# Expert matmuls as four column strips while attention runs

## The chip, the cores and the metric

The kernel runs on one core of one Trainium2 chip. The metric is the device time of one execution in microseconds (us), the median of several runs. TensorE (PE in the profile) multiplies matrices: a weight load puts a block into its 128x128 array, a matmul streams columns through it and writes to PSUM, the accumulation memory. The array can also be used as several smaller tiles side by side: in the text *full* is the whole array (128x128), *rows* are four tiles of 32x128, *columns* are four tiles of 128x32, and there are eighths of 32x64 and 64x32. VectorE (DVE) and ScalarE (ACT) do elementwise work, GpSimd (POOL) and SyncE (SP) mainly issue transfers (DMAs).

## The reference

Attention over 8 batches, 12 heads, 448 tokens and 64 dimensions of a head, followed by one expert layer over all 3584 tokens:

```python
scores = scale * np.matmul(q, k.transpose(0, 1, 3, 2))
scores = scores - np.max(scores, axis=-1, keepdims=True)
attn = np.exp(scores)
attn = attn / (np.sum(attn, axis=-1, keepdims=True) + 1e-09)
attn_out = np.matmul(attn, v)
...
x = attn_out.transpose(0, 2, 1, 3).reshape(B * S, H * D)   # 3584 x 768
h = x @ w_in                                               # 768 x 2048
g = h * (1.0 / (1.0 + np.exp(-h)))
out = g @ w_out                                            # 2048 x 768
```

## The kernel before, in words

**Units.** Attention is cut into units of one batch and four heads (three groups of heads a batch); batch 0 is cut once more, into pieces of 224 query tokens, so its first units are half as wide. For a unit, `scores` (L339, matmul at L327) makes the transposed scores of keys against queries on row tiles, the head in the row position; ACT takes the exponential (`expo`, L364); `attend` (L414) multiplies the exponentials by ones, which gives the sums, and by V, in column tiles with the head in the column position (matmuls at L390 and, for sums of a pair of units, L406). DVE inverts the sums and writes the scaled result as `xT` (L473), the expert layer's input with the model dimension on the partitions.

**Expert layer.** `ffn1` (L484, matmul at L487) makes one block of 128 hidden units for all tokens of a piece: six matmuls that accumulate over the model dimension, 224 columns wide for the two pieces of batch 0 and 448 for the later batches. ACT takes tanh, DVE forms the gate `G` (L533). `plain` (L695, matmul at L699) and `product` (L675, matmul at L685) multiply `G` by `w_out` in matmuls of 384 columns; `product` belongs to a scheme for pairs of token blocks that needs seven products in place of eight, with sums and differences made by DVE (L671, L746). The last two batches have the same scheme for `w_in`: `pair_product` (matmul at L622), which comes after attention. All these matmuls use the full array.

**Order.** The order on PE, ACT and DVE is not written out by hand. The class `Order` (L78) is a planner that runs while the kernel is built: it keeps a clock, books each operation with an assumed duration, and at each step starts what is ready by its rules. Scores go first, one burst each `PACE` (2.6), the value passes and expert operations fill the time between them; rings stand for buffers. The operations are then recorded in that order, so a change of an assumed duration can change the order. `on_pe` (L106) adds `SWITCH` (0.094) to an operation whose `mode` (the tile) differs from the one before it; `run_qk` names its mode "rows" or "rest rows", `run_av` "cols" (and leaves "rest cols" behind after a pair of units), expert operations "full". Until the first expert operation PE multiplies zeros in idle time (`run_zeros`, L1434), with `warm["on"]` set.

**Program.** Each matmul is recorded with a weight load of its own. The built program has 3,679 matmuls on PE and 7,407 instructions in all there. PE's instructions come from memory over a DMA queue of their own (queue 8 in the profile).

Of the kernel before, what the change touches and what calls it, by code (L numbers as in the profile page):

```python
# [25 lines left out]
def mm(n):  # L26
    return n / 2400.0 + 0.0026
# [6 lines left out]
class Ring:  # L34


    def __init__(self, n):
        self.free = [0.0] * n
# [26 lines left out]
class Op:  # L65


    def __init__(self, eng, busy, emit, deps=(), bias=0.0, tail=HOP, then=None):
        self.eng, self.busy, self.emit = eng, busy, emit
        self.deps, self.bias, self.tail, self.then = list(deps), bias, tail, then  # L70
        self.done = None
        self.half = False

    def ready(self):
        return when(self.deps)


class Order:  # L78


    def __init__(self, shy):
        self.now, self.shy = 0.0, shy
        self.free = {"PE": 1.0, "ACT": 2.1, "DVE": 1.2, "POOL": 1.2}
        self.wait = {"ACT": [], "DVE": []}
        self.pool = []
        self.dma_free = 0.0
        self.out = []
        self.mode = None
        self.busy = {e: 0.0 for e in self.free}

    def add(self, op):
# [4 lines left out]
        self.out.append((self.now, len(self.out), fn))  # L96

    def start(self, op):
        self.emit(op.emit)
        self.free[op.eng] = self.now + op.busy  # L100
        self.busy[op.eng] += op.busy
        op.done = self.now + op.busy + op.tail
        if op.then:
            op.then(op.done)

    def on_pe(self, op, mode):  # L106
        gap = SWITCH if mode != self.mode else 0.0
        self.mode = mode
        op.busy += gap
        self.start(op)  # L110
# [55 lines left out]
def kernel(  # L166
# [9 lines left out]
    nc = tc.nc  # L176
# [135 lines left out]
    def turn_q(n):  # L312
        t = rawq[n][:].bitcast(FP32).rearrange("p (g i) -> p g i", i=32)
        nc.vector.transpose(out=t, in_=t)  # L314
        QT[n] = rawq[n].rearrange("p (q e) -> p e q", e=2)

    def score_banks(n, w, ys):
        for y in ys:
            pS_t[(n, w, y)] = ps.tile(
                [128, 2, 512], FP32, name=f"s_{n}_{w}_{y}", tag="s", bufs=2  # L320
            )
# [139 lines left out]
    def x3(b, cc):  # L461
        if (b, cc // 3) not in xT:
            xT[(b, cc // 3)] = sb.tile(
                [128, 3, S], FP16, name=f"xT_{b}_{cc // 3}", tag="xT", bufs=NX3
            )
        return xT[(b, cc // 3)]
# [17 lines left out]
    def ffn1(b, f, t0, t1):  # L484
        h = ps.tile([128, 512], FP32, name=f"h_{b}_{f}_{t0}", tag="m", bufs=4)
        for cc in range(NDC):
            nc.tensor.matmul(  # L487
                out=h[:, 0 : t1 - t0],
                lhsT=w_in_t[:, cc, 128 * f : 128 * (f + 1)],
                rhs=x3(b, cc)[:, cc % 3, t0:t1],  # L490
                start=(cc == 0),
                stop=(cc == NDC - 1),
            )
        h_t[(b, f, t0)] = h
# [87 lines left out]
    def w_in_part(i, j, f0, f1):  # L582
        at = DFF // 2 * j
        return w_in_t[:, 3 * i : 3 * i + 3, at + 128 * f0 : at + 128 * f1]
# [18 lines left out]
    def pair_product(f, m):  # L603
        if m in (1, 5):
            pp_t[(f, PBANK[m])] = ps.tile(
                [128, 512], FP32, name=f"f_{f}_{m}", tag="m", bufs=4
            )[:, 0:S]
        elif m == 6:
            two = ps.tile([128, 2, 512], FP32, name=f"f_{f}_{m}", tag="s", bufs=2)
            pp_t[(f, "B")], pp_t[(f, "D")] = two[:, 0, 0:S], two[:, 1, 0:S]  # L610
        x = {(r, i): x3(PB + r, 3 * i) for r in range(2) for i in range(2)}
        lo, at = f // 4 * 4, slice(128 * (f % 4), 128 * (f % 4 + 1))
        a, w = {
            1: (x[0, 0], w_in_part(0, 0, f, f + 1)),
            2: (x[0, 1], w_in_part(1, 0, f, f + 1)),
            3: (sx_t.get(4), w_in_part(1, 1, f, f + 1)),
        }.get(m, (None, None))
        if a is None:
            i = {4: 4, 5: 1, 6: 2, 7: 3}[m]
            a, w = x[1, 1] if m == 4 else sx_t[i], tw_t[(i, lo)][:, :, at]  # L620
        for c in range(3):
            nc.tensor.matmul(  # L622
                out=pp_t[(f, PBANK[m])],
                lhsT=w[:, c, :],
                rhs=a[:, c, :],
                start=(c == 0 and m in (1, 6, 5)),
                stop=(c == 2),
                skip_group_check=True,
            )
# [45 lines left out]
    def product(qd, m):  # L675
        a, b = 2 * qd, 2 * qd + 1
        if m in (5, 6):
            w = S_t[(qd, m - 4)]
        else:
            t, i = {1: (a, 0), 2: (a, 1), 3: (a, 1), 7: (b, 0), 4: (b, 1)}[m]  # L680
            w = rows(t, i)
        if BANK[m] == m:
            pr_t[(qd, m)] = ps.tile([128, 512], FP32, name=f"p_{qd}_{m}", tag="m", bufs=4)
        for f in range(HF):
            nc.tensor.matmul(  # L685
                out=pr_t[(qd, BANK[m])][:, 0:OH],
                lhsT=w[:, f, :],
                rhs=W_[m][:, f, :],
                start=(f == 0 and BANK[m] == m),
                stop=(f == HF - 1),  # L690
                skip_group_check=True,
            )


    def plain(t, j, f0, f1):  # L695
        if f0 == 0:
            pr_t[("o", t, j)] = ps.tile([128, 512], FP32, name=f"o_{t}_{j}", tag="m", bufs=4)
        for f in range(f0, f1):
            nc.tensor.matmul(  # L699
                out=pr_t[("o", t, j)][:, 0:OH],  # L700
                lhsT=rows(t, f // HF)[:, f % HF, :],
                rhs=B_[f // HF, j][:, f % HF, :],
                start=(f == 0),
                stop=(f == NFF - 1),
                skip_group_check=True,
            )
# [56 lines left out]
    od = Order(SHY)  # L763
# [476 lines left out]
    qk_seq, av_seq = [], []  # L1240
# [191 lines left out]
    warm = {"on": 1, "first": 1}  # L1432
# [10 lines left out]
    while True:  # L1443
        plan_turns(qk_seq[0][0][0] + 3 if qk_seq else NU)
        plan_adds()
        plan_pair()
        plan_sums()
        soon = od.step()
        if od.free["PE"] <= od.now:
            ran = False  # L1450
            moe_i, moe_next = moe_ready()
            av_data["at"] = None
            qk, av = qk_at(), av_at()
            wait = av_data["at"]
            if wait is not None and wait <= od.now - 1000 and not (av is not None and av <= od.now):
                moe_i, moe_next = moe_ready(0)
                soon.append(min([x for x in m_ring.free if x>od.now] or [od.now+0.1]))
            near = qk_seq and units[qk_seq[0][0][0]][0] == 0 and qk is not None
            near = near and qk < od.now + NEAR
            if qk is not None and qk <= od.now and (od.now >= pace["next"] or moe_i is None):  # L1460
                u0 = units[qk_seq[0][0][0]]
                pace["next"] = min(max(pace["next"], od.now - 4), od.now) + (
                    PACE if u0[0] > EAGER else 0.0
                ) * len(qk_seq[0][2]) / 2
                run_qk()
                od.now, keep = od.free["PE"], od.now
                while u0[0] and (a := av_at()) is not None and a <= od.now:
                    run_av()
                    od.now = od.free["PE"]
                od.now = keep  # L1470
                ran = True
            elif near:
                pass
            elif moe_i is None and av is not None and av <= od.now:
                run_av()
                ran = True
            elif moe_i is not None:
                if av is not None and av <= od.now - 0:
                    run_av()
                else:  # L1480
                    moe.pop(moe_i)[2]()
                ran = True
            if not ran:
                soon += [x for x in (moe_next, qk, av, pace["next"]) if x is not None]
        soon.append(od.free["PE"])
        later = [x for x in soon if x > od.now]
        if not later:
            break
        wait = min(later) - od.now
        if warm["on"] and od.free["PE"] <= od.now and wait > 0.06 and od.now > 0.9:  # L1490
            each = mm(128) if od.now > COLD else 0.107
            n = max(1, int((wait - 0.06) / each), int(wait / each + 0.9) * (od.now < COLD))
            if warm.pop("first", None):
                n = FIRST
            od.on_pe(Op("PE", n * each, lambda n=n: run_zeros(n)), "full")
        od.now = min(later)
        assert od.now < 2000.0
# [33 lines left out]
```

## Time and profile before

| | |
|---|---|
| median of 3 runs | 396.07 us (395.69 to 396.17) |
| the profiled execution | 396.11 us |
| its span | 394.3 us |
| TensorE clock granted | 1.00 |
| PE busy | 387.6 us |
| DVE, ACT, POOL busy | 272.7, 253.6, 83.6 us |
| DMA packets | 35,579, 34.43 MB |

The span is the time from the first to the last instruction that the profiler saw. Busy time of PE is modelled: matmuls overlap, so their starts tell more than their durations; "x32" after a group counts its instructions. "PEld" are weight loads. A wait's releaser is what ended it; "issue" means that nothing in the profile did. The DMA share is the mean busy share of 16 DMA engines, and may read a little above one.

The four costliest groups of PE, by line and tile (busy us, mean ns of one, idle time before them):

```
L487 PE MATMUL h<-xT,w_in_t 128*128 128x448 f16 x480 | 98.9, 353 | 0.0
L685 PE MATMUL p<-w_out_t,G 128*128 128x384 f16 x368 | 65.3, 326 | 0.3 <-DVE xT L473 0.2
L685 PE MATMUL p<-D,S 128*128 128x384 f16 x208 | 37.4, 327 | 0.0
L327 PE MATMUL s<-rq,KT 32*128 32x448 f16 x496 | 36.0, 360 | 0.1
```

### The profile page before, as it was taken

What the parts mean: (1) busy time and instruction counts of PE and PEld (TensorE: products, weight loads), DVE (VectorE), ACT (ScalarE), POOL (GpSimd) and SP (SyncE); (2) the same over time, 40 slices, a digit from 0 to 9 for tenths busy, and PEclk for the clock granted to TensorE, in tenths of its full rate; (3) what the DMA queues carried; (4) which work ended last, traced back from release to release, by engine and by line L of the source; (5) the groups of instructions that cost most, each with busy time, mean ns of one, the idle gap of its engine ahead of it and who ended that gap; (6) DMA issues with size and microseconds to landing.
All of it is one profiled execution on the core that took longest, in us unless ns stands there. A gap on an engine that the chain in (4) does not pass through costs nothing.

```text
span 394.3 us, 9242 instructions
## 1 busy us (share of the span) xinstructions
PE 387.6 (98%) x3679; PEld 200.0 (51%) x3679; DVE 272.7 (69%) x570; ACT 253.6 (64%) x404; POOL 83.6 (21%) x153
## 2 busy tenths in 40 slices
PE   8999999999999999999999999999999999999995
PEld 7667764443444444554444444444444555555563
DVE  2466676999967588963698576896879945457332
ACT  4988885696871986753974759867685236763221
POOL 7532547215001532330006131600000000000000
PEclk9999999999999999999999999999999999999999
DMA  7999999919033946292016683711100130001343
GB/s 116 204 210 210 162 179 187 154 35 141 13 65 79 148 56 86 50 193 62 2 23 90 116 162 52 98 24 31 51 2 7 33 99 25 2 1 29 95 110 90
DMA packets 35579, 34.43 MB, mean 87 GB/s; under 512 B 11600, under 2 KB 34000, under 8 KB 35536
## 3 DMA queue, kind: packets, MB, share of 16 engines
q0 software_dynamic: 24784, 22.82, 38.7%
q1 hardware_dynamic: 9984, 10.24, 9.6%
q10 hardware_dynamic: 768, 0.79, 0.8%
q8 instruction: 29, 0.48, 0.5%
q14 instruction: 14, 0.11, 0.1%
HBM read 45.61 MB, written 11.01 MB: 144 GB/s over the span
## 4 chain that ended last, share of the span: by engine, by line
PE 91%; DVE 4%; ACT 1%; DMA 1%; issue 1%; ACTq 0%; POOL 0%; DVEq 0%; POOLq 0%
PE p L685 28%; PE h L487 28%; PE s L327 12%; PE a L390 10%; PE f L622 8%; PE o L699 3%; PE a L406 2%; DMA rq<-in_q_dram 1%; DVE tw L598 1%; ACT E L364 1%; PE z L1438 1%; DVE G L533 1%; ACTq L734 0%; DVE S L671 0%; DVE G L671 0%
## 5 line engine op out<-in xcount | busy, mean ns | idle before, releaser
L364 ACT ACTIVATE E<-s 128x896 f16<-128x896 f32 (+1 forms) x172 | 149.9, 915 | 22.6 <-PE s L327 21.2
L487 PE MATMUL h<-xT,w_in_t 128*128 128x448 f16 (+1 forms) x672 | 118.9, 327 | 0.0
L487 PEld LDWEIGHTS <-w_in_t 128*128 128x128 f16 x672 | 61.1, 98 | 54.4 <-issue 18.8
L498 ACT ACTIVATE th<-h 128x448 f16<-128x448 f32 (+1 forms) x112 | 54.3, 495 | 31.6 <-PE h L487 21.5
L533 DVE SCALAR_TENSOR_TENSOR G<-th,h 128x448 f16<-128x448 f16 (+2 forms) x112 | 55.1, 507 | 16.0 <-ACT th L498 14.0
L685 PE MATMUL p<-w_out_t,G 128*128 128x384 f16 x368 | 65.3, 326 | 0.3 <-DVE xT L473 0.2
L685 PEld LDWEIGHTS <-G 128*128 128x128 f16 x472 | 45.3, 98 | 33.4 <-issue 4.0
L269 POOL DMA_DIRECT2D V<-in_v_dram x88 | 48.6, 570 | 57.1 <-PE a L390 43.6
L327 PE MATMUL s<-rq,KT 32*128 32x448 f16 (+4 forms) x864 | 56.7, 340 | 0.6 <-ACT E L364 0.4
L742 ACT COPY ost<-p 128x384 f32<-128x384 f32 x39 | 18.7, 479 | 48.5 <-PE p L685 33.5
L390 PE MATMUL a<-E,V 128*32 128x448 f16 (+3 forms) x864 | 40.6, 335 | 0.0
L473 DVE SCALAR_TENSOR_TENSOR xT<-a,rdn 128x448 f16<-128x448 f32 (+1 forms) x54 | 28.9, 568 | 12.5 <-PE a L390 11.7
L254 POOL DMA_DIRECT2D rq<-in_q_dram x27 | 15.2, 561 | 105.2 <-PE s L327 85.8
L685 PE MATMUL p<-D,S 128*128 128x384 f16 x208 | 37.4, 327 | 0.0
L327 PEld LDWEIGHTS <-KT 32*128 32x128 f16 (+2 forms) x864 | 17.5, 98 | 28.7 <-issue 25.9
L390 PEld LDWEIGHTS <-V 128*32 128x32 f16 (+2 forms) x864 | 18.2, 95 | 22.6 <-issue 15.3
L375 DVE TENSOR_TENSOR T<-T,E 128x1792 f16<-128x1792 f16 x20 | 21.7, 1086 | 11.4 <-ACT E L364 11.4
L685 PEld LDWEIGHTS <-S 128*128 128x128 f16 x208 | 19.4, 98 | 16.2 <-issue 3.1
L375 DVE TENSOR_TENSOR T<-E,E 128x1792 f16<-128x1792 f16 x20 | 21.7, 1083 | 7.8 <-ACT E L364 7.8
L647 ACT ACTIVATE G<-f 128x448 f16<-128x448 f32 x32 | 16.2, 547 | 8.4 <-PE f L622 8.3
L304 DVE STREAM_TRANSPOSE KT<-rk 128x256 f32<-128x256 f32 (+3 forms) x48 | 16.6, 384 | 5.9 <-DMA rk<-in_k_dram 5.8
L314 DVE STREAM_TRANSPOSE rq<-rq 128x448 f32<-128x448 f32 (+1 forms) x27 | 15.3, 570 | 6.0 <-DMA rq<-in_q_dram 5.9
(124 smaller groups left out, 323.6 us busy)
## 6 DMA issues: line engine op xcount, KB each, us to landing
out_dram<-ost SPq DMA_DIRECT2D x208, 48.0 KB, 1.6
rk<-in_k_dram POOLq DMA_DIRECT2D x24, 224.0 KB, 4.9
rq<-in_q_dram POOLq DMA_DIRECT2D x21, 224.0 KB, 5.2
w_in_t<-in_moe_w_in_dram POOLq DMA_DIRECT2D x6, 512.0 KB, 11.6
w_out_t<-in_moe_w_out_dram POOLq DMA_DIRECT2D x4, 768.0 KB, 12.9
V<-in_v_dram POOLq DMA_DIRECT2D x43, 64.0 KB, 3.8
V<-in_v_dram POOLq DMA_DIRECT2D x40, 48.0 KB, 3.6
out_dram<-ost ACTq DMA_DIRECT2D x16, 48.0 KB, 1.8
```

The source lines that it names most:

```text
L269: nc.gpsimd.dma_start(out=VT[b][32 * x : 32 * (x + 1), hs, 0:count, :], in_=v[b, hs].rearrange("h (i g) d -> i h g d", g=TPP)[:, :, first ...
L327: nc.tensor.matmul(out=pS[p0 : p0 + 32 * (x1 - x0), h % 2, at : at + nq], lhsT=KT[(b, hg)][32 * h : 32 * (h + 1), c, x0:x1, :, e], rhs=QT[ ...
L364: nc.scalar.activation(out=E[(n, w)][0:kr, 2 * y : 2 * y + 2, 0:nk], in_=pS_t[(n, w, y)][0:kr, :, 0:nk], func=AF.Exp, scale=attn_scale,)
L375: nc.vector.tensor_tensor(out=T[n], in0=T[n] if step else E[(n, 0)], in1=E[(n, step + 1)], op=ALU.add,)
L390: nc.tensor.matmul(out=a[32 * h : 32 * (h + 1), 0:nq], lhsT=w, rhs=e[k0:k1, h, at : at + nq], start=start, stop=stop,)
L473: nc.vector.scalar_tensor_tensor(out=x3(b, cc)[:, cc % 3, 32 * g0 : 32 * g1], in0=acc[(n, part)][:, 0:nq], scalar=0.5, in1=rdn_t[n].rearra ...
L487: nc.tensor.matmul(out=h[:, 0 : t1 - t0], lhsT=w_in_t[:, cc, 128 * f : 128 * (f + 1)], rhs=x3(b, cc)[:, cc % 3, t0:t1], start=(cc == 0), s ...
L498: nc.scalar.activation(out=th, in_=h_t[(b, f, t0)][:, 0 : t1 - t0], func=AF.Tanh)
L533: nc.vector.scalar_tensor_tensor(out=dst[:, f, at + lo : at + hi], in0=th_t[(b, f, t0)][:, lo - t0 : hi - t0], scalar=1.0, in1=h_t[(b, f, ...
L622: nc.tensor.matmul(out=pp_t[(f, PBANK[m])], lhsT=w[:, c, :], rhs=a[:, c, :], start=(c == 0 and m in (1, 6, 5)), stop=(c == 2), skip_group_ ...
L685: nc.tensor.matmul(out=pr_t[(qd, BANK[m])][:, 0:OH], lhsT=w[:, f, :], rhs=W_[m][:, f, :], start=(f == 0 and BANK[m] == m), stop=(f == HF - 1),
L742: nc.scalar.copy(out=ost(qd, i, j), in_=bank(qd, m))
```

## The change

A helper `wide` issues a matmul either as it was or as four, each with a quarter of the stationary columns and of the output partitions, on 128x32 tiles; all four stream the same operand, and together they do the same arithmetic. It takes the place of the matmul in `ffn1`, `pair_product`, `product` and `plain`. An operation gets its `strips` mark in `on_pe`: when its mode is "full" and attention work is left (`od.attention`, set anew at each step of the planner), the mode becomes "cols", so that the planner books no change of tile between it and a value pass. When the operations are recorded, `run` sets the flag that `wide` reads. The order is drawn anew with these modes.

```diff
@@ class Op
         self.done = None
         self.half = False
+        self.strips = False
@@ class Order
         self.out = []
         self.mode = None
+        self.strips = False
+        self.attention = True
         self.busy = {e: 0.0 for e in self.free}
...
     def start(self, op):
-        self.emit(op.emit)
+        self.emit(lambda: self.run(op))
...
+    def run(self, op):
+        self.strips = op.strips
+        op.emit()
+
     def on_pe(self, op, mode):
+        if mode == "full" and self.attention:
+            mode, op.strips = "cols", True
         gap = SWITCH if mode != self.mode else 0.0
         self.mode = mode
         op.busy += gap
...
+    def wide(out, lhsT, rhs, **flags):
+        n = 4 if od.strips else 1
+        for j in range(n):
+            at = slice(128 // n * j, 128 // n * (j + 1))
+            nc.tensor.matmul(out=out[at], lhsT=lhsT[:, at], rhs=rhs, **flags)
+
@@ ffn1; the same in pair_product, product and plain
         for cc in range(NDC):
-            nc.tensor.matmul(
+            wide(
                 out=h[:, 0 : t1 - t0],
                 lhsT=w_in_t[:, cc, 128 * f : 128 * (f + 1)],
                 rhs=x3(b, cc)[:, cc % 3, t0:t1],
@@ the planner's loop
         plan_pair()
         plan_sums()
+        od.attention = bool(qk_seq or av_seq) and not warm["on"]
         soon = od.step()
```

More of the change, by code (lines that the diff above doesn't have):

```diff
@@ L621, in pair_product @@
         for c in range(3):
-            nc.tensor.matmul(
+            wide(
                 out=pp_t[(f, PBANK[m])],
@@ L684, in product @@
         for f in range(HF):
-            nc.tensor.matmul(
+            wide(
                 out=pr_t[(qd, BANK[m])][:, 0:OH],
@@ L698, in plain @@
         for f in range(f0, f1):
-            nc.tensor.matmul(
+            wide(
                 out=pr_t[("o", t, j)][:, 0:OH],
```

## The prediction

> **What bounds the kernel now.** I read the busy shares first, then the chain of waits, then TensorE's waits and timeline, and last the DMA queues and the packets of one of them.
>
> ```profile
> PE 387.6 (98%) x3679; PEld 200.0 (51%) x3679; DVE 272.7 (69%) x570; ACT 253.6 (64%) x404; POOL 83.6 (21%) x153
> ...
> PE 91%; DVE 4%; ACT 1%; DMA 1%; issue 1%; ACTq 0%; POOL 0%; DVEq 0%; POOLq 0%
> ...
> q8 instruction: 29, 0.48, 0.5%
> ```
>
> TensorE (PE) is busy 98% of the 394.3 us span and is 91% of the chain that ended last; the next engine has 31% to spare. So a microsecond taken from or put on PE is a microsecond of the time. The view of PE's waits agrees: four entries, 2.1 us together. The last line is queue 8, which brings PE's own program: 0.48 MB in 29 packets of 16,384 bytes; the built program has 7,407 PE instructions, so a packet holds 256 of 64 bytes.
>
> What the change aims at is in PE's timeline around 70 us (start, duration, what):
>
> ```profile
> 67.92 1.47 PE L699 MATMUL o<-w_out_t,G 128*128 128x384 f16 x8
> 69.32 1.63 PE L390 MATMUL a<-E,V 128*32 128x448 f16 x32
> 70.89 0.58 PE L327 MATMUL s<-rq,KT 32*128 32x448 f16 x8
> 71.39 0.82 PE L699 MATMUL o<-w_out_t,G 128*128 128x384 f16 x4
> ```
>
> Starts are to be compared with starts. Eight matmuls of 384 columns take 8 x 0.1626 = 1.30 us (0.1626 us is the start-to-start time within such a run), yet the value pass starts 1.40 us after them: 0.10 us went to the change of tile. The four-matmul run at 71.39 starts 0.50 us after the scores, whose two rounds need 0.38 and some 0.02 us of their own: 0.10 us again. I took the same difference at every change of tile in the trace. Medians in ns: full to rows (32x128, scores) 96, rows to full 107, full to columns (128x32, values) 93, columns to full 106, rows to columns 102, columns to rows 106, columns to 64x32 103, 64x32 to full 127, 64x32 to columns 124. Which two tiles meet hardly matters; how often they change does.
>
> The third thing is a place where PE waited for nothing that another engine did (timeline of PE, and the busy time of PE in three stretches with clock, DMA share and GB/s):
>
> ```profile
> 27.39 0.56 PE L390 MATMUL a<-E,ones 128*32 128x224 f16 x13
> 28.43 0.28 PE L390 MATMUL a<-E,ones 96*32 96x224 f16 x3 [0.49 <-issue]
> ```
>
> ```profile
> 16.87:22.24 5.37, 5.37 (x132) 1.00 1.13 210
> 22.24:28.43 6.19, 5.71 (x134) 1.00 1.13 211
> 28.43:34.48 6.05, 6.04 (x127) 1.00 1.13 210
> ```
>
> Sixteen matmuls belong to one pass; 13 run, and the last three come 0.65 us late in the middle of a group of four, released by "issue". The packets of queue 8 around it started at 19.85, 26.02 and 32.12 us and took 0.95, 0.95 and 0.94 us. Late in the kernel packets start when PE has run some 170 to 190 instructions past a multiple of 256; the stall sits at instruction 962, which is 194 past one. So I read it as a block boundary: PE had run out of program, and the packet that ended at 26.97 us ended the stall 1.47 us later. From the stall's end (PE enters the new block and asks for the next) to the next packet's start are 3.69 us. One round of supply is thus 3.69 + 0.94 + 1.47 = 6.1 us for 256 instructions. The three stretches are the blocks there: 5.37, 6.19 and 6.05 us. The kernel before touches this limit only here, where scores and value passes of 224 columns stand close together; later its blocks last 10 to 24 us, since a full-array matmul of 448 columns is two instructions in 0.189 us.
>
> **The change part by part.**
>
> Array time. Four strips of 128x32 in four column groups should take the time of one full matmul. The value passes show it: in the run at 69.32 the groups of four start 0.189 us apart, as full matmuls of 448 columns do. I cost 480 + 480 matmuls of 448 and 384 columns at no change. The 186 matmuls of 224 columns become groups of four that the first value passes run at 95 to 100 ns against 96: 0 to +0.7 us; I take 0, because in those stretches the supply below decides.
>
> Changes of tile. Counted in the two built orders: 259 before, 236 after. Between expert work and value passes 40 changes (14 + 12 + 14) become 4, but 64x32 to columns rises from 5 to 18, and around scores nothing is saved: full-rows pairs turn into columns-rows pairs. With the medians above (neighbours where a pair is new) the sums are 26.9 and 25.0 us: **-1.9 us**. The bounds by the cheapest and dearest row, 23 x 0.089 and 23 x 0.127, are -2.0 and -2.9; I take -1.9, pair by pair.
>
> The redrawn order. Up to about 60 us the orders agree; later the same work is shifted by a few operations, and attention runs up to 2 us earlier against the pair sums of w_out. No step is added on ACT, DVE, POOL or SP; POOL's and SP's issues have the same counts. The wait of PE that a new order can win or lose is bounded by the 3.5 us that all waits and late starts cost before: I take 0, with -1 to +2 for the range.
>
> Instructions. This is the dear part. PE's program grows from 7,407 to 14,283 instructions (3,438 matmuls more, each with its weight load), so 56 packets instead of 29. The 0.44 MB are nothing beside 34.43 MB; their rate matters. I cut the new order into blocks of 256 and gave each its array time from the rows above. Until 28.4 us the order is the old one, stall included. Then follow the first two sets of expert matmuls, 224 columns wide, where a group of eight instructions needs only 0.096 us. The nine blocks from there need 4.43, 3.50, 3.50, 4.18, 3.50, 3.50, 4.36, 4.84 and 5.15 us of array time, 37.0 together. At 6.1 us a block the supply needs 54.9: +17.9 us. Nothing covers it: PE is what sets the end, and exponentials and gates are only late with it. The page has the DMA engines at 9 tenths until 79 us, so the 6.1 us measured in that load applies at first; but the stretch now lasts from 28 to some 80 us with the same bytes to load. Behind it a block (eight instructions per 0.163 or 0.189 us, plus scores and changes of tile) needs 5.3 to 6.6 us, and the DMA share falls from 1.13 to 0.45 (80 to 280 us). The shortest round that I can read is that of the packets at 12.27 and 19.85 us: each starts 2.98 us after PE passed the boundary, 2.98 + 0.95 + 1.47 = 5.4 us. So I take 0 for the later blocks, with +2.1 if the round stayed at 6.1. For the early ones I let the last four rounds be 5.4 us: 17.9 - 4 x 0.7 = **+15.1 us**. Bounds, each block's shortfall added up: 5.0 us throughout, an estimate a little below the shortest, gives +7; 6.4 gives +20.
>
> [...]
>
> Sum: -1.9 + 15.1 = +13.2, span 394.3 to 407.5. That execution took 396.11 us, 1.8 us around its span, beside a median of 396.07. So 409.3: **409 us**.
>
> **The rivals.**
>
> An issue floor instead of late blocks: PE's sequencer cannot pass a matmul with its load faster than the densest stretch, 5.37 us / 132 = 41 ns. Groups of four then last at least 163 ns: nothing for 448 and 384 columns, 186 x 0.067 = +12.5 us for 224. With -1.9 that is 406.7. For it: no stretch of several us is denser. Against it: shorter runs are (112 instructions in 1.6 us, 29 ns a matmul), and the stall came in one piece.
>
> [...]
>
> No limit of supply: the 0.65 us was a single accident, and blocks are fetched far enough ahead. Then only the changes of tile count: 396.1 - 1.9 = **394.2 us**, faster. For it: one visible stall in 29 packets. Against it: three rounds in a row that all come out near 6 us, and a stall on a boundary. It would decide if a round were under 3.5 us.
>
> The strips don't run at once, since all four stream the same operand: each group would take four times as long, hundreds of us. Four value strips stream four different operands at full rate, so I see no reason.
>
> **How the numbers follow.** Late blocks 0.79 (own range 401 to 418), issue floor 0.07, no limit 0.11, strips in series 0.01, and 0.02 for a small loss of supply that cancels the gain. What this kernel's measurement can tell from no change is about 0.2%, 0.8 us. Faster 0.11; same 0.02; slower 0.87. The range takes the late blocks with their bounds and the issue floor: 396.1 - 1.9 + 7 = 401 to 396.1 - 1.9 + 20 + 2 + 2 = 418.
>
> **What would show it.** PE's busy count near 7,117 matmuls and queue 8 at about 56 packets. Right, if between 28 and 85 us PE has gaps of 1 to 3 us released by "issue" every 256 instructions, packets of queue 8 some 6 us apart, and expert work there takes 12 to 18 us longer, while behind it the two kernels run side by side. Evenly spread groups of 163 ns without gaps would be the issue floor. No gaps, and a value pass starting straight behind strips without its 0.1 us, would be the second rival. Wrong in size, if the rounds are 5 us or reach into the later stages.

## The result, and the profile after

The changed kernel takes 407.36 us (median of 4 runs, 405.36 to 408.87) beside 395.88 us of the kernel before in the same runs: a ratio of 1.0283, 95% interval 1.0259 to 1.0308. It is slower, as forecast, by 11.5 us where 13 were forecast. The profiled execution is the shortest of the four, 405.36 us with a span of 403.6.

The page of the changed kernel; the lines answer to those shown of before (busy time, chain by engine, PE's program queue):

```profile
PE 387.0 (96%) x7117; PEld 209.6 (52%) x7117; DVE 273.5 (68%) x570; ACT 253.1 (63%) x404; POOL 83.6 (21%) x153
...
q8 instruction: 55, 0.90, 1.0%
...
PE 89%; DVE 4%; issue 3%; ACT 1%; DMA 1%; ACTq 0%; DVEq 0%; POOLq 0%
```

PE works as long as before (387.0 against 387.6 us), with nearly twice as many matmuls; the span is 9.3 us longer, and "issue" has grown from 1% to 3% of the chain. PE's program now comes in 55 packets instead of 29. Where the time went is in the timeline of PE, changed kernel, in the stretch of the 224-column strips (start, duration, what, count, idle time before):

```profile
34.30 0.85 PE L330 MATMUL h<-xT,w_in_t 128*32 128x224 f16 x26 [1.22 <-issue]
35.09 0.57 PE L342 MATMUL s<-rq,KT 32*128 32x448 f16 x8
35.59 2.48 PE L330 MATMUL h<-xT,w_in_t 128*32 128x224 f16 x94
40.23 0.85 PE L330 MATMUL h<-xT,w_in_t 128*32 128x224 f16 x26 [2.16 <-issue]
```

At 35.59 us 94 strips run back to back, at 0.096 us for four, the spacing of one full-array matmul of 224 columns in the kernel before. Then PE stands still for 2.16 us in the middle of a group of four (94 and 26 are 120, five operations of 24), and nothing that another engine did releases it. Scores are hit in the same way:

```profile
57.72 0.57 PE L342 MATMUL s<-rq,KT 32*128 32x448 f16 x6
60.90 0.37 PE L342 MATMUL s<-rq,KT 32*128 32x448 f16 x2 [2.61 <-issue]
```

I counted PE's matmuls and weight loads up to each such place, and measured each against the undisturbed spacing of its row. There are seven between 27 and 66 us, of 0.39, 1.39, 2.33, 2.30, 0.47, 2.78 and 0.74 us, 10.4 us together. They stand behind instructions 961, 1217, 1473, 1729, 2241, 2497 and 2753 of PE, 256 or 512 apart; so in each, PE stops after instruction 193 or 194 of a block of 256, and it goes on 1.30 to 1.55 us after the end of a packet of queue 8. The kernel before has one, of 0.65 us, at the same count.

What the change was to save is saved. Timeline of PE, changed kernel:

```profile
78.51 0.83 PE L330 MATMUL o<-w_out_t,G 128*32 128x384 f16 x16
79.17 1.62 PE L405 MATMUL a<-E,V 128*32 128x448 f16 x32
```

Four groups of 384 columns need 4 x 0.1626 = 0.65 us, and the value pass starts 0.66 us after them. Before, it started 0.10 us later than its work explained. At 21 places of this trace where strips and a pass on 128x32 tiles meet, in either order, the median of the extra time is 0.00 us.

The account of the two profiled executions (405.36 - 396.11 = 9.25 us): stalls on program 10.4 - 0.65 = +9.7; changes of tile -1.9 by count and medians; a wait of the pair products of w_out for xT near 316 us 1.23 instead of 0.32, +0.9; the first scores, near 6 us, wait for the transposed queries 0.65 us instead of 0.26, but start only 0.10 us later than before, +0.1. Together +8.8; some 0.4 us are not accounted for.

### The profile page after: what moved, and what is told of

Same layout as the page of the kernel before. It is cut to its first block, busy times and chain, and to the rows that moved or that the text cites. A ratio compares the mean times of both kernels' runs of the same rounds, so it can differ in the third digit from the quotient of the medians.

```text
span 403.6 us, 16126 instructions
## 1 busy us (share of the span) xinstructions
PE 387.0 (96%) x7117; PEld 209.6 (52%) x7117; DVE 273.5 (68%) x570; ACT 253.1 (63%) x404; POOL 83.6 (21%) x153
## 4 chain that ended last, share of the span: by engine, by line
PE 89%; DVE 4%; issue 3%; ACT 1%; DMA 1%; ACTq 0%; DVEq 0%; POOLq 0%
PE p L330 27%; PE h L330 27%; PE s L342 12%; PE a L405 10%; PE f L330 8%; PE o L330 3%; PE a L421 1%; DMA rk<-in_k_dram 1%; ACT E L379 1%; DVE tw L613 1%; PE z L1453 1%; DVE G L548 1%; DVE S L686 1%; DVE G L686 0%; DVE xT L488 0%
## 5 line engine op out<-in xcount | busy, mean ns | idle before, releaser
L330 PE MATMUL h<-xT,w_in_t 128*32 128x448 f16 (+2 forms) x2670 | 120.1, 327 | 6.1 <-issue 6.1
L330 PEld LDWEIGHTS <-w_in_t 128*32 128x32 f16 (+1 forms) x2742 | 72.9, 97 | 62.4 <-issue 22.3
L330 PEld LDWEIGHTS <-G 128*32 128x32 f16 (+1 forms) x1544 | 53.8, 97 | 37.8 <-issue 7.6
L330 PE MATMUL p<-w_out_t,G 128*32 128x384 f16 (+1 forms) x1016 | 65.2, 326 | 1.2 <-DVE xT L488 1.1
L263 POOL DMA_DIRECT2D rq<-in_q_dram x27 | 15.1, 558 | 116.4 <-PE s L342 102.3
L330 PE MATMUL p<-D,S 128*32 128x384 f16 (+1 forms) x568 | 37.4, 326 | 0.0
L330 PEld LDWEIGHTS <-S 128*32 128x32 f16 (+1 forms) x568 | 20.9, 97 | 13.7 <-issue 1.6
L330 PE MATMUL p<-D,G 128*32 128x384 f16 (+1 forms) x272 | 19.1, 326 | 0.0
```

The lines of the kernel that those rows point to most:

```text
L330: nc.tensor.matmul(out=out[at], lhsT=lhsT[:, at], rhs=rhs, **flags)
```

## The experiments

Eleven kernels. Those that keep the changed kernel's order differ from it only where the diff says so.

### The order alone

Strips are booked, and every matmul is recorded on the full array:

```diff
     def run(self, op):
-        self.strips = op.strips
+        self.strips = False
         op.emit()
```

> The redrawn order of the changed kernel, but every expert matmul on the full array again: 3,679 matmuls, 258 changes of tile (before 259). Late blocks of program (my theory: PE's instructions come in blocks of 256, one about every 6 us while the DMA engines are loaded, and the strips of 224 columns use a block up in 3.5 us): no block is shorter than in the kernel before, so 395 to 397.5 us; up to 1 us more than before is the order's own, since the changed kernel has one wait of 1.1 us for xT near 316 us that before has at 0.2. Rival, the order is what costs: 404 us or more.

Measured 396.72 us, ratio 1.0020 (1.0011 to 1.0030). The redrawn order costs 0.8 us and not 11. PE's waits in this kernel (engine, line, what it waited for: us in total, times, longest) name the place:

```profile
PE p L330 <- DVE xT L488: 0.9, 1, 0.9
```

The kernel before has the same entry at 0.2: the last product before `pair_product` comes earlier than its input.

### The strips alone, in the order before

```diff
     def on_pe(self, op, mode):
         if mode == "full" and self.attention:
-            mode, op.strips = "cols", True
+            op.strips = True
```

> Strips as in the changed kernel, but the planner books them as full, so that the order is that of before; 7,093 matmuls, 236 changes of tile. Late blocks: -1.9 us of changes of tile, some 8 to 12 us of stalls at instruction 193 or 194 of a block between 28 and 70 us: 402 to 408 us. Rival, the order is what costs: 394 us.

Measured 405.90 us, 1.0258 (1.0237 to 1.0278): the loss is there without the new order. Stalls stand again at 193 or 194 of a block, 8.1 us in six of them. The built program has 236 changes of tile too, so the new order had saved no change of tile. Its profile shows a second cost, in the section on the hardware below.

### Strips only where they are wide, and only where they are narrow

The changed kernel's order. `op.narrow` is set in `queue_ffn1` for the pieces of 224 tokens; the second kernel has `and op.narrow`.

```diff
     def run(self, op):
-        self.strips = op.strips
+        self.strips = op.strips and not op.narrow
         op.emit()
```

> The changed kernel's order; strips for the matmuls of 448 and 384 columns (3,840 strips in 960 groups), full array for the 186 of 224 columns, so PE's program is 13,100 instructions long instead of 14,283 and 239 changes of tile are left. Late blocks: the blocks under 5 us are gone (shortest behind 60 us 5.2), so the 10.4 us of stalls are nearly gone: 394.5 to 397 us, below the kernel before by up to 1.6 unless the order's wait takes it back. Rival, each strip costs a little wherever it stands: 84% of the loss stays, about 405 us.

> The complement: the changed kernel's order, strips for the matmuls of 224 columns alone (744 strips), everything else on the full array: 4,237 matmuls, 257 changes of tile. Late blocks: seven blocks of 3.5 to 4.4 us from 28 us on, shortfall to a 6.1 us round 16.0 us, to the rounds that the changed kernel had about 9: 402 to 408 us, with a stall at instruction 193 or 194 of nearly every block. Rival, each strip costs a little: 16% of the loss, 398.5 us.

Wide strips alone: 395.20 us, 0.9985 (0.9977 to 0.9994), a little below the kernel before, with 3,840 of the 4,584 strips of the changed kernel. Narrow strips alone, the other 744: 408.16 us, 1.0301 (1.0287 to 1.0315), just above the expected stretch. So the whole loss belongs to a sixth of the strips, and a price on each strip is refuted. The timeline of PE in the kernel with narrow strips alone:

```profile
36.24 2.48 PE L331 MATMUL h<-xT,w_in_t 128*32 128x224 f16 x94
40.87 1.49 PE L331 MATMUL h<-xT,w_in_t 128*32 128x224 f16 x26 [2.16 <-issue]
```

The same 94 strips and the same 2.16 us as in the changed kernel: later strips have no part in it. The wide ones use up 256 instructions in 5.2 us at the least, and no stall on program stands in their stretch.

### Strips only where they meet a value pass

A pass over the finished order turns a run of strips back to the full array when neither neighbour is on 128x32 tiles; the number of changes stays 236. `od.pe` lists each operation of PE with the tile ahead of it and behind it; the lines that fill it are left out here.

```diff
...
+    i = 0
+    while i < len(od.pe):
+        j = i
+        while j < len(od.pe) and od.pe[j][0].strips:
+            j += 1
+        if j > i and od.pe[i - 1][2] != "cols" and od.pe[j][1] != "cols":
+            for x in od.pe[i:j]:
+                x[0].strips = False
+        i = j + 1
```

> The changed kernel's order; a run of expert operations is issued as strips only where it stands next to a value pass on 128x32 tiles, elsewhere on the full array: 236 changes of tile as in the changed kernel, but 4,669 matmuls instead of 7,117. Late blocks: one block of 4.4 us near 28 us costs about 1.5 us, the rest is 5.4 us or more: 394 to 396.5 us. Rival, each strip costs a little: 29% of the loss, 397.5 us. Rival, fewer changes of tile are worth nothing: 396 to 398.

Measured 396.05 us, 1.0000 (0.9991 to 1.0009). By count and medians it saves 2.2 us of changes of tile. It gives back 0.8 us for the order, and its profiled run has one stall of 1.4 us at 32.8 us, at instruction 193 of a block: narrow strips beside a value pass of batch 0 were left. (The stall at 28.4 us, 0.65 us in the kernel before, is 0.15 here.) Some 0.5 us that should be left over are not accounted for. The time lies in the stretch of the theory and in that of the second rival, so this run alone doesn't tell whether fewer changes of tile are worth anything; the next two do.

### Both lessons together

Order of before and no narrow strips; in the second kernel also only runs that meet a value pass.

> Strips for the matmuls of 448 and 384 columns alone, recorded in the order of the kernel before (the planner books them as full): 239 changes of tile, 1.6 us less than before by the medians; no block under 5.15 us. Late blocks, and the order's own loss of 0.8 us: 394.3 us (393.8 to 394.9), 0.9 below the same strips in the new order. Rival, the rest of the gain is eaten by something in the strips themselves: 395 us or more.

> Order of before; strips only in runs next to a value pass and none of 224 columns: 4,417 matmuls, 238 changes of tile, 2.0 us less than before by the medians, no block under 5.5 us but those of before. Late blocks: 393.9 us (393.4 to 394.6), as the strips that touch no value pass saved nothing. Rival, the saving of a change of tile is less than its median gap: 395 us.

Wide strips in the old order: 394.85 us, 0.9966 (0.9954 to 0.9978), at the upper end of what was expected. Only those that touch: **394.26 us, 0.9951 (0.9938 to 0.9964)**, below both kernels. Of 2.0 us expected by the medians 1.9 came. With 3,808 strips instead of 984 the gain is 0.6 us smaller. Of this 0.4 us were expected by the medians (1.6 against 2.0): going from columns to the rows of the scores takes 106 ns in the trace of before where going from the full array takes 96, and many of the added strips meet scores. The other 0.2 us is within the intervals. The profiled execution of the faster kernel is not one of its typical ones: it took 398.09 us, and the last section shows at what clock. The saving at one place, timeline of PE with wide strips in the old order:

```profile
67.69 1.48 PE L331 MATMUL o<-w_out_t,G 128*32 128x384 f16 x32
69.00 1.62 PE L406 MATMUL a<-E,V 128*32 128x448 f16 x32
```

The value pass starts 1.31 us after the eight products; in the kernel before it was 1.40.

### Is it the DMA traffic?

Dense strips deep in the kernel, where little is transferred: the kernel before with `ffn1` of batch 3 alone in strips of 224 columns, eight in place of one matmul, so that six blocks last 3.3 to 5.1 us.

```diff
         for cc in range(NDC):
+            for x0 in (t0, t0 + S // 2) if b == DENSE else (t0,):
+                x1 = x0 + S // 2 if b == DENSE else t1
+                for j in range(4 if b == DENSE else 1):
+                    p0, p1 = (32 * j, 32 * (j + 1)) if b == DENSE else (0, 128)
                     nc.tensor.matmul(
-                out=h[:, 0 : t1 - t0],
+                        out=h[p0:p1, x0 - t0 : x1 - t0],
...
-                start=(cc == 0),
+                        start=(cc == 0 and x0 == t0),
```

> The kernel before, with the expert matmuls of batch 3 alone (near 180 to 205 us, where the DMA share is about 0.45) issued as strips of 224 columns, eight in place of one: 4,351 matmuls, 261 changes of tile. Six blocks of 3.3 to 5.1 us in a stretch with light DMA traffic. If a round takes 6.1 us whatever the traffic: 36.6 - 23.2 us and less what the queue holds ahead, +11 to +13: 407 to 409 us. If the round is set by the DMA traffic (my theory): rounds of 3.5 to 5 us, 0.5 to 1.5 us a block, 398 to 402 us, with stalls again at instruction 193 or 194 of a block.

> The kernel before with the expert matmuls of batch 3 as strips of 224 columns, without added traffic (dense_light once more, with the accumulation of both halves begun once; dense_light lost the first of six terms in half of its columns). Control for the next two: 396.6 us, no stall inside a group between 175 and 210 us, packets of queue 8 some 3.6 us apart there.

The first has `start=(cc == 0)` for both halves and so leaves out the first of six terms in half of its columns; it issues the same matmuls. Measured 396.64 us, 1.0009 (0.9999 to 1.0019), and 396.49 us, 1.0011 (1.0001 to 1.0021). I had expected 398 to 402 of the first, so it is a miss: there are no stalls at all. Packets of queue 8 come every 3.5 to 4.2 us there and PE never waits. A round of 6 us is thus no constant.

Then the missing ingredient was added, 32 copies on SP's queue to output rows that are overwritten later, to the kernel before and to the dense one:

```diff
         h_t[(b, f, t0)] = h
+        if b == 3:
+            r0 = 6 * S + 128 * (f % 7)
+            for c0 in (0, OH):
+                nc.sync.dma_start(
+                    out=out[r0 : r0 + 128, c0 : c0 + OH],
+                    in_=moe_w_out[128 * f : 128 * (f + 1), c0 : c0 + OH],
+                )
```

> The kernel before, with 32 copies of 196 KB from w_out to rows of the output that are overwritten later, issued on SP's queue about where batch 3's expert matmuls stand. Control for what the traffic alone does: blocks last over 10 us there, so no late block; 396 to 399 us, the stores behind the copies being late.

> Both: batch 3's expert matmuls as strips of 224 columns, and the copies. If traffic on the DMA engines is what makes a round of supply long: stalls of 1 to 3 us at instruction 193 or 194 of a block while the copies run (DMA share near 1), packets of queue 8 5 to 7 us apart, 3 to 10 us above the larger of the two controls. If the early stretch is special for another reason: no stalls, and no more than the sum of both controls.

Measured 398.24 us, 1.0052 (1.0035 to 1.0070), and 401.35 us, 1.0121 (1.0102 to 1.0140): 3.1 us above the larger control and 2.6 above the sum of both extra times. PE at the same place, first dense strips alone, then with the copies:

```profile
196.25 0.60 PE L328 MATMUL s<-rq,KT 32*64 32x448 f16 x16
196.78 2.48 PE L492 MATMUL h<-xT,w_in_t 128*32 128x224 f16 x96
199.20 0.57 PE L328 MATMUL s<-rq,KT 32*128 32x448 f16 x8
```

```profile
196.15 0.60 PE L328 MATMUL s<-rq,KT 32*64 32x448 f16 x16
196.69 0.95 PE L492 MATMUL h<-xT,w_in_t 128*32 128x224 f16 x32
198.92 1.33 PE L492 MATMUL h<-xT,w_in_t 128*32 128x224 f16 x48 [1.28 <-issue]
```

And PE in ten-microsecond stretches (length, busy time and instructions, clock, DMA share, GB/s), again first without and then with the copies:

```profile
185.00:195.00 10.00, 10.00 (x366) 1.00 0.07 19
195.00:205.00 10.00, 10.00 (x344) 1.00 0.17 27
```

```profile
185.00:195.00 10.00, 10.00 (x370) 1.00 0.57 157
195.00:205.00 10.00, 8.40 (x288) 1.00 0.54 135
```

Same instructions, same place; with the DMA engines at 0.54 to 0.57 instead of 0.07 to 0.17 PE stops twice, for 1.45 and 0.49 us, both times at instruction 194 of a block and 1.43 and 1.33 us after the end of a packet. From PE's entry into a block to the start of the next packet passed 0.2 to 0.7 us in the six dense blocks from 186 us on without the copies; with them it was up to 2.4 us. The copies on the full-array kernel give no such stall. That traffic makes the round long is shown; the packets before these two stalls came 4.5 to 4.9 us after the ones ahead of them, not 5 to 7. The two stalls are 1.9 of the 2.6 us. Beside them value passes wait for ACT's output buffers in both kernels (1.0 us in the control, 1.4 with the strips), and scores wait 1.2 us more for exponentials; together that is more than 2.6, so how much each adds stays open.

## Why the prediction was right, and where it was off

**Direction and mechanism** held. The time of 407.36 us lies 1.6 us below the forecast, inside its own range. PE sets the end; the stalls stand on block boundaries, "released by issue", in the stretch that was named, and behind it the kernels run side by side but for the wait for xT. The signs held in part: the gaps end at 66 us and not 85, one boundary among them has none, the packets there came 3.4 to 6.7 us apart, and the stalls behind 28.4 us add up to 10 us where 12 to 18 were named. That the number came so close is partly luck. The largest term was 5.4 us too large, and 3.0 us that were not in the sum (1.0 us of waits, and 2.0 us between the profiled run and the median) made up for more than half of it.

**Array time.** Right: four strips last as long as one full matmul, at 224 columns too (0.096 us in the runs of 94).

**Changes of tile.** Right: -1.9 us by count, and the two kernels with the old order and no more late blocks than before gained 1.3 and 1.9 us. The saving needed no new order. The bounds beside it were misread: the cheapest change in the prediction's list is 93 ns, not 89, which gives -2.1 and not -2.0.

**The redrawn order.** Taken as 0 with -1 to +2; it costs 0.8 us (`order_only`).

**Instructions.** The mechanism was right and the size off. The step was 6.1 us for five rounds and 5.4 for four, +15.1 us; the profiled run had +9.7. The nine blocks from 28.4 us lasted 5.95, 5.92, 5.92, 4.13, 4.15, 6.47, 5.30, 4.80 and 5.20 us. So 6.1 was well measured for the first three, and wrong as a constant afterwards. (Its lower bound was added up wrongly too: the shortfalls to 5.0 us a block make 8.2 us, not 7.) PE in stretches of the changed kernel (length, busy, instructions, clock, DMA share, GB/s):

```profile
28.36:46.15 17.79, 12.28 (x384) 1.00 1.17 205
46.15:54.33 8.18, 7.97 (x256) 1.00 0.91 120
54.33:66.20 11.87, 8.59 (x255) 1.00 1.20 199
66.20:75.00 8.80, 8.80 (x227) 1.00 0.23 35
```

The last two columns go with the rounds: 5.9 us at a share of 1.17, short enough for blocks of 4.1 us at 0.91 and 120 GB/s, 5.3 to 6.5 at 1.20, and no stall at 0.23. The share alone tells little: with the copies, packets came 4.5 to 4.9 us apart at only 0.54 to 0.57, but at 135 to 157 GB/s. I had taken the DMA load from the page as 9 tenths up to 79 us. The tenths hide a lull that the kernel before has in the same place:

```profile
46.15:54.33 8.18, 8.11 (x103) 1.00 0.95 127
```

So two of the blocks that were given 6.1 us could have been seen to stand in lighter traffic. Only from 66 us on do the two kernels differ in load (before: 1.02, 188 GB/s).

**What was not in the sum.** The profiled run has 2.0 us less than the median, and it is the only one of the four at a granted clock of 1.00; the others show 0.99. The last section shows what such a clock can come from; for these three runs it isn't shown.

**The rivals.** The issue floor is refuted: groups of 224 columns run at 0.096 us, which is 24 ns a matmul, and the loss is in gaps. The same row refutes strips that run one after the other. "No limit of supply" is refuted for the change as it stands, and is what the kernels without narrow strips look like, 394.26 us at best against the 394.2 of that rival. That blocks are fetched far enough ahead holds for the wide strips, at 395.2 us with blocks of 5.2 us and more and no stall among them; it fails for the narrow ones, with stalls of up to 2.8 us for blocks of 3.5.

## What to carry to other kernels

Here instructions had to be fetched: the narrow strips alone, 744 at equal array time, made the 396.72 us of `order_only` into 408.16. Where a rewrite multiplies instructions at equal array time, divide the new order into blocks (256 instructions here, one packet of 16,384 bytes) and compare each block's time with the spacing of the program queue's packets under that stretch's DMA load. Read that load in GB/s over windows as short as a few blocks; here the tenths of the page hid a lull to 127 GB/s. The stalls counted here, with "issue" as releaser and in the middle of a group or pass, all at instruction 193 or 194 of a block, were late program and no dependency: in the changed kernel each ended 1.30 to 1.55 us after the end of a packet. And a saving that is made at a boundary should be paid for at that boundary only: strips next to value passes brought the gain (394.26 us with 984 strips), the others brought instructions and no gain that these runs can tell (394.85 with 3,808).

## What the runs showed of the hardware that was not expected

Behind some waits of PE the granted clock halved. PE in four stretches of 3.4 us, kernel with the strips in the old order (clock is the third figure behind the stretch):

```profile
34.40:37.80 3.40, 3.40 (x128) 1.00 1.16 210
37.80:41.20 3.40, 0.97 (x36) 1.00 1.16 211
41.20:44.60 3.40, 3.40 (x69) 0.50 1.16 207
44.60:48.00 3.40, 2.82 (x96) 1.00 0.99 122
```

PE stood still for 2.43 us within one stretch of 3.41 us, and in the next the granted clock was 0.50: 69 matmuls instead of some 130. The trace has a second such drop at 61.66 us, 3.41 us long, behind a stall of 2.06 us; the kernel with narrow strips alone has two as well. In the profiled executions of before and after, the two changes of the granted clock lie 389.12 and 399.36 us apart, 114 and 117 times 3.4133 us, and the drop at 61.66 us lasted one such step. Cut at such steps, counted in each trace from a change of its clock, the stretches ahead of the four drops hold 2.05 to 2.43 us of idle time. In the profiled run of the changed kernel the stalls of 2.1 to 2.6 us lie across the edges of such steps; its most idle stretch holds 1.88 us, and no drop follows:

```profile
42.48:45.90 3.42, 1.53 (x65) 1.00 1.24 188
45.90:49.31 3.41, 3.16 (x110) 1.00 0.77 85
```

Idle time alone doesn't decide, though. In the profiled execution of the fastest kernel (strips next to value passes, none narrow) PE waited 1.11 us for transposed queries, with no stall on program, and the clock was 0.50 for the next two stretches:

```profile
24.92:28.33 3.41, 2.30 (x57) 1.00 1.13 212
28.33:31.75 3.42, 3.42 (x53) 0.50 1.12 211
31.75:35.16 3.41, 3.41 (x50) 0.50 1.12 208
```

This goes with 398.09 us where the kernel's median is 394.26. Why the shorter wait was enough no run here settles. Drops like these would fit the three other runs of the changed kernel, 1.3 to 3.5 us longer at 0.99, but those have no trace here. Behind the first drop in the old order the next block was late anyway (its stall is 0.74 us, 2.30 in the changed kernel), so that drop cost less than the 1.7 us of work that it took.

Supply of program has a second delay, which varied little: PE went on 1.30 to 1.55 us after the end of the awaited packet in the seven stalls of the changed kernel, 1.47 us in the one of the kernel before, and 1.43 and 1.33 us with the copies. What varies is the time from PE's entry into a block, which I take for the request for the next, to the next packet's start: 1.12 to 4.15 us by the stalls of the changed kernel. What that time goes to no trace here tells.
